# A fifth ranked job transposed, and four row blocks' gate logits from bfloat16 parts made by GpSimd

## The chip, the core and the metric

The kernel runs on one core of a Trainium2 chip. The metric is the device time of one execution in microseconds, the median of several runs. A core has TensorE (matmuls, with an instruction that loads weights beside them), VectorE, ScalarE and GpSimd, which work side by side on the on-chip memory SBUF and on the banks PSUM into which TensorE writes, and SyncE, which issues the direct loads. The tables call them PE, PEld, DVE, ACT, POOL and SP.

## What is computed

Chunked attention, then a layer of eight experts that takes the best two for each token, then a layer of eight experts that takes the best one, with a capacity:

```
x = attention(q, k, v, mem_k, mem_v)             # 1536 tokens x 512
logits = x @ w_gate + log1p(exp(x @ w_noise)) * noise
for e in 8 experts:                              # each token goes to its best two
    h = relu(x[mask] @ w1[e])                    # 512 -> 1024
    out[mask] += weight * (h @ w2[e])            # 1024 -> 512
logits = out @ w_gate2                           # second layer: the best one only
expert = argmax(logits); weight = softmax(logits)[expert]
out2[i] = weight * (relu(out[i] @ v1[expert]) @ v2[expert])   # first 384 tokens of an expert
```

The second gate picks by a maximum, so its logits have to be as exact as float32 makes them. A row of `out` is the sum of two experts' rows, and so are its logits.

## The kernel before

**Jobs.** After the attention stage the kernel runs jobs one after the other. A job is one expert's rows with its two layers. `V0` is a small block of the first rows in plain float32, and `V8` is an expert whose rows are known early (312 rows). `S0` to `S6` are the other seven experts of the first layer, sorted by their load while the kernel runs, with room for 432, 412, 404, 396, 384, 384 and 384 rows. `U0`, `UL` and `R0` to `R6` are the jobs of the second layer. `run_jobs` goes through them; `units()` of the class `Job` lists a job's units of work, and TensorE meets them in that order. Between units, `due` puts in the splits of weights that a plan gives for this unit, the blocks of the next job's input (`x_block`), and hooks such as the start of a gather.

**Three products for one.** A matmul of a job is made of three: weights and rows are each split into a high and a low part (`whi` and `wlo`, `xh` and `xl`, `hh` and `hl`), and `mm3` (L850 to L861) adds high by high, high by low and low by high. `split` (L785 to L798) makes the weights' parts: ScalarE copies a quarter of a block of 512 columns to the high part (L795), and VectorE subtracts it for the low part (L796); for the pieces named in `job.pool` GpSimd subtracts in its place. For V8 this is piece 3 of each weight block. The first layer's result gets its high part from ScalarE (`hh`, L872) and its low part from VectorE (`hl`, L873). The weights themselves come by SyncE's queue in halves (`half`, L764 to L776).

**Two kinds of job.** Kind "W" keeps the result transposed: layer 2 has eight units, one for each 128 of the 512 columns and half of the layer, its result is copied to `yh` (ScalarE, L888) and `yl` (VectorE, L889), and later `y_block` (L1055 to L1074) takes each block of 128 rows through eight matmuls of 144 columns, 128 of which turn it back into rows and 16 of which are the gate's logits. These blocks come in the next job's first layer, one behind a unit. Kind "M" makes rows directly: `rows2` for each block of 128 rows in two halves, then `weighted` (L1012) multiplies each row by its weight, `row_columns` (L1022) transposes the block by four matmuls (L1027) and ScalarE copies it to `yt` (L1028), `row_logits` (L1030) takes four float32 products for the logits (L1034), VectorE copies them beside the row (L1035), and `scatter` (L1037) lets GpSimd start the indirect transfer that adds the block to the table of rows (L1041). `Job.rows` (L1138) puts the two steps `row_columns` and `put` on a list, `todo`, from which `run_jobs` takes one after each unit.

**Which job is what.** A ranked job is "W" where its room is over 384, so S0 to S3 are; S4, S5 and S6 are "M". V0 is "T", a third kind of one block in float32.

**What stands around S4.** At its end `job.late` runs `overflow_done`: the queue of routing steps is emptied, and all engines read a counter and branch (L1278 to L1281) over a loop, `rest1`, for rows that did not find room. The loop is not run with these inputs. It uses the buffers `st["y"]` (`yh`, `yl`) and the PSUM bank A. A hook at S5's unit 3 starts `choose`, whose loads tell which experts the second layer has.

## Time and profile before

| | us |
|---|---|
| median of three runs | 598.04 |
| lowest and highest of these | 596.28 and 598.69 |
| the profiled execution | 597.38 |
| its span, first to last instruction | 595.5 |
| TensorE busy, matmuls | 582.8 (98%) |
| TensorE busy, weight loads | 519.4 (87%) |
| VectorE busy | 369.9 (62%) |
| ScalarE busy | 303.6 (51%) |
| GpSimd busy | 171.9 (29%) |

The profile is one execution on the chip. An engine is busy while it runs an instruction that computes; branches, semaphores and the issue of DMAs are not counted. The shares are averages over the whole span, over stages with different limits. TensorE's granted clock was 0.999 of its full 2.4 GHz over the span. A float32 matmul is recorded as two instructions, so the four float32 products of a block's logits are eight records.

In the rows below, a line of the trace names the line of the kernel, the engine's operation, the result and the operands (`wlo<-raww,whi`), and the shape as partitions by elements. L796 is the line 796 that the listing above shows. Where a row says what ended a wait, the operation behind the arrow is the one that was waited for.

### The profile page before, as it was taken

Reading aid. Unit: us, or ns where it says so; the run is one execution under the profiler, and the core shown is the slowest. Engines: PE = TensorE matmul, PEld = TensorE weight load, DVE = VectorE, ACT = ScalarE, POOL = GpSimd, SP = SyncE. Lnnn points to the kernel's source line nnn. Section 1 sums busy time; section 2 is a strip of 40 time slices with the busy share of each in tenths; the row PEclk is TensorE's granted clock in tenths of the full one; section 3 lists DMA queues with packets and bytes.
Section 4 is the critical chain, followed back from the end, with each engine's and each line's share of the span. In section 5 each row is a group of like instructions: output and inputs, shape, how many; then the busy total and the mean of one; then the engine's idle time right before and its main releaser. Section 6 shows DMA issues by size and latency. Waiting matters only on the chain. (4 is left out here: it accounts for less than half of the span.)

```text
span 595.5 us, 12285 instructions
## 1 busy us (share of the span) xinstructions
PE 582.8 (98%) x4547; PEld 519.4 (87%) x4547; DVE 369.9 (62%) x977; ACT 303.6 (51%) x638; POOL 171.9 (29%) x248
## 2 busy tenths in 40 slices
PE   8999999999999999999999999999999999999996
PEld 5798766899999999999998898988979978879984
DVE  7788757966466555555555257373668648457662
ACT  5764534355455445445355345344327657467562
POOL 8896104245114114213030311203341111220110
PEclk9999999999999999999999999999999999999999
DMA  9995747365767648556455563544376576975750
GB/s 263 281 203 157 250 138 245 113 214 168 228 202 184 199 155 213 165 140 165 143 122 162 134 166 138 110 143 125 40 249 221 193 263 227 390 265 175 249 175 25
DMA packets 75293, 110.13 MB, mean 185 GB/s; under 512 B 28083, under 2 KB 28083, under 8 KB 75226
## 3 DMA queue, kind: packets, MB, share of 16 engines
q1 hardware_dynamic: 65866, 84.72, 44.9%
q0 software_dynamic: 9360, 24.54, 17.6%
q8 instruction: 38, 0.62, 0.5%
q14 instruction: 29, 0.24, 0.1%
HBM read 88.63 MB, written 20.48 MB: 183 GB/s over the span
## 5 line engine op out<-in xcount | busy, mean ns | idle before, releaser
L796 DVE TENSOR_TENSOR wlo<-raww,whi 128x512 fp32r<-128x512 f32 x223 | 149.5, 693 | 39.2 <-ACT whi L795 37.6
L795 ACT ACTIVATE whi<-raww 128x512 fp32r<-128x512 f32 x228 | 135.6, 623 | 3.3 <-SPq L1372 1.4
L873 DVE SCALAR_TENSOR_TENSOR hl<-psA,hh 128x256 fp32r<-128x256 f32 (+7 forms) x104 | 53.4, 514 | 77.1 <-ACT hh L872 76.8
L872 ACT ACTIVATE hh<-psA 128x256 fp32r<-128x256 f32 (+7 forms) x104 | 47.4, 455 | 102.3 <-PE psA L861 102.0
L861 PE MATMUL psA<-xh,wlo 128*128 128x256 f32 (+7 forms) x416 | 84.8, 325 | 2.0 <-DVE hl L873 1.0
L861 PE MATMUL psA<-xl,whi 128*128 128x256 f32 (+7 forms) x416 | 82.2, 319 | 0.0
L861 PE MATMUL psA<-xh,whi 128*128 128x256 f32 (+7 forms) x416 | 82.2, 319 | 0.0
L1041 POOL DMA_INDIRECT x_rows<-yr,ids x25 | 39.3, 1571 | 123.6 <-ACT whi L795 86.2
L861 PEld LDWEIGHTS psA<-xh,wlo 128*128 128x128 f32 x416 | 66.5, 188 | 4.2 <-DVE hl L873 2.2
L861 PEld LDWEIGHTS psA<-xl,whi 128*128 128x128 f32 x416 | 68.1, 188 | 0.5 <-DVE xl L813 0.2
L861 PEld LDWEIGHTS psA<-xh,whi 128*128 128x128 f32 x416 | 68.2, 188 | 0.3
L801 POOL DMA_INDIRECT xg<-x_rows,ids x37 | 37.2, 1005 | 95.4 <-DVE gs L1081 39.8
L861 PE MATMUL psC<-wlo,hh 128*128 128x512 f32 (+1 forms) x184 | 52.7, 406 | 0.0
L861 PE MATMUL psC<-whi,hh 128*128 128x512 f32 (+1 forms) x184 | 51.3, 396 | 0.0
L861 PE MATMUL psC<-whi,hl 128*128 128x512 f32 (+1 forms) x184 | 50.1, 394 | 0.0
L813 DVE TENSOR_TENSOR xl<-psB,xh 128x512 fp32r<-128x512 f32 (+4 forms) x32 | 20.4, 638 | 35.8 <-ACT xh L812 35.7
L861 PEld LDWEIGHTS psC<-whi,hl 128*128 128x128 f32 (+1 forms) x184 | 34.1, 186 | 8.1
L861 PEld LDWEIGHTS psC<-whi,hh 128*128 128x128 f32 (+1 forms) x184 | 33.8, 186 | 8.1
L861 PE MATMUL psA<-hh,wlo 128*128 128x312 f32 (+4 forms) x160 | 37.0, 352 | 0.1
L1048 POOL DMA_INDIRECT out_dram<-yr,oids x12 | 11.9, 994 | 87.1 <-ACT yr L1017 53.6
L861 PEld LDWEIGHTS psC<-wlo,hh 128*128 128x128 f32 (+1 forms) x184 | 32.1, 186 | 5.6
L812 ACT ACTIVATE xh<-psB 128x512 fp32r<-128x512 f32 (+4 forms) x32 | 17.8, 555 | 37.6 <-PE psB L809 35.4
(371 smaller groups left out, 935.2 us busy)
## 6 DMA issues: line engine op xcount, KB each, us to landing
raww<-in_moe_w_dram SPq DMA_DIRECT2D x114, 512.0 KB
raw<-in_k_dram SPq DMA_DIRECT2D x6, 512.0 KB
raw<-in_q_dram SPq DMA_DIRECT2D x6, 512.0 KB
x_rows<-xs SPq DMA_DIRECT2D x12, 256.0 KB
out_dram<-zero SPq DMA_DIRECT2D x3, 1024.0 KB
...
```

What stands on the lines that cost most here:

```text
L795: nc.scalar.activation(hi[:, c], raw, AF.Copy)
L796: (eng or nc.vector).tensor_tensor(lo[:, c], raw, hi[:, c], op=OP.subtract)
L801: return nc.gpsimd.indirect_dma_start(out=xg, out_offset=None, in_=src, in_offset=bass.IndirectOffsetOnAxis(ap=ids_ap, axis=0))
L812: nc.scalar.activation(xh[:, :, o], pv[:, :, 0:n], AF.Copy)
L813: low = lambda: nc.vector.tensor_tensor(xl[:, :, o], pv[:, :, 0:n], xh[:, :, o], op=OP.subtract)
L861: nc.tensor.matmul(ps, w[a], x[b], start=first and i == 0, stop=last and i == n - 1)
L872: nc.scalar.activation(hh[:, f, 0:C], ps[:, 0:C], AF.Relu)
L873: nc.vector.scalar_tensor_tensor(hl[:, f, 0:C], ps[:, 0:C], 0.0, hh[:, f, 0:C], op0=OP.max, op1=OP.subtract)
L1041: wr = nc.gpsimd.indirect_dma_start(out=x2_d, out_offset=off, in_=yr[:n], in_offset=None, compute_op=OP.add)
L1048: wr = nc.gpsimd.indirect_dma_start(out=out, out_offset=off, in_=yr[:n, 0:DM], in_offset=None, bounds_check=N - 1, oob_is_err=False)
```

## The change

It has three parts.

1. **S4 becomes transposed.** The first five ranked jobs are "W", whatever their room. S4's row blocks then go through `y_block` in S5's first layer, behind the branch. As `yh` and `yl` hold S4's result across the branch, `rest1` gets two buffers of its own and the PSUM bank C. The hook that starts `choose` moves from S5's unit 3 to its unit 5.
2. **Four blocks' logits from three bfloat16 parts.** For V0's block, for two blocks of S5 and for the first of S6 (`job.parts`), the transposed rows in `yt` are split by `three` into three bfloat16 parts: a cast, a subtraction to a remainder, a cast of that, and a second subtraction, each on 128x512, all on GpSimd. The gate's weights get the same three parts once, in `wg3`, side by side in 24 columns. Twelve matmuls (three parts by four pieces of 128) with 24 columns take the place of the four float32 products, and one reduction by VectorE of the three sums in place of its copy. The parts lie where `hr` was, the remainder in `h0`, which hold a part of V0 and are free behind it. For such a block `put` moves: it is kept until just before the next block's transposes, or, for the last of them, two empty entries stand between the transposes and `put`.
3. **V8's weights.** `V8.pool` goes from `(3,)` to `(1, 3)`: GpSimd subtracts two of the four pieces of each of V8's weight blocks.

```diff
--- before.py
+++ after.py
@@ -197,6 +197,8 @@
     noi = axp.tile([128, NT, V], F32, name="noi")
     wg1 = consts.tile([128, KD, 2 * V], F32, name="wg1")
     wg2 = consts.tile([128, KD, E], F32, name="wg2")
+    wg3 = consts.tile([128, KD, 3 * E], BF, name="wg3")
+    wgr = consts.tile([128, KD, E], F32, name="wgr")
 
     def xs(t):
         if t not in xb:
@@ -401,6 +403,14 @@
             nc.vector.tensor_copy(yid[:, :, i, 128:136], wg2)
         nc.vector.tensor_tensor(yid[:, :, 0, 136:144], wg2, yid[:, :, 0, 128:136], op=OP.subtract)
         nc.vector.tensor_copy(yid[:, :, 1, 136:144], zero[:, 0:32].rearrange("p (k e) -> p k e", k=KD))
+        three([wg3[:, :, E * i:E * i + E] for i in range(3)], wg2, wgr)
+
+    def three(b, x, r):
+
+        nc.gpsimd.tensor_copy(b[0], x)
+        nc.gpsimd.tensor_tensor(r, x, b[0], op=OP.subtract)
+        nc.gpsimd.tensor_copy(b[1], r)
+        nc.gpsimd.tensor_tensor(b[2], r, b[1], op=OP.subtract)
 
     def all_of(gen):
 
@@ -1019,17 +1029,27 @@
             nc.vector.tensor_scalar(yr[:n, m:DM], ps[:n, m:DM], g[:n], None, op0=OP.mult)
         return yr
 
-    def row_columns(yr, n):
+    def row_columns(yr, n, parts=False):
 
         p = bank("B")
         pv = p.rearrange("p (k n) -> p k n", k=KD)
         for k in range(KD):
             nc.tensor.transpose(pv[:, k, 0:n], yr[:n, 128 * k:128 * k + 128], ident[:n, :n])
         nc.scalar.activation(st["yt"][:, :, 0:n], pv[:, :, 0:n], AF.Copy)
-
-    def row_logits(yr, n):
+        if parts:
+            three(st["y3"], st["yt"], st["h0"][0])
+
+    def row_logits(yr, n, parts=False):
 
         p = bank("D")
+        if parts:
+            for k in range(KD):
+                for i in range(3):
+                    nc.tensor.matmul(p[:n, 0:3 * E], st["y3"][i][:, k, 0:n], wg3[:, k],
+                                     start=k + i == 0, stop=k == KD - 1 and i == 2)
+            nc.vector.tensor_reduce(yr[:n, DM:W2], p[:n, 0:3 * E].rearrange("p (s e) -> p e s", s=3),
+                                    axis=AX.X, op=OP.add)
+            return
         for k in range(KD):
             nc.tensor.matmul(p[:n, 0:E], st["yt"][:, k, 0:n], wg2[:, k], start=k == 0, stop=k == KD - 1)
         nc.vector.tensor_copy(yr[:n, DM:W2], p[:n, 0:E])
@@ -1107,6 +1127,8 @@
             self.pool = ()
             self.weigh = 1 if kind == "T" else 5
             self.prev = []
+            self.parts = 0
+            self.put = None
             self.g = []
 
         def fetch(self):
@@ -1148,10 +1170,21 @@
             n = min(128, self.C - 128 * blk)
             yr = weighted(st["l2"], self.g[blk], n, self is R[-1])
             if self.first:
+                parts = blk < self.parts
+
                 def put():
-                    row_logits(yr, n)
+                    row_logits(yr, n, parts)
                     scatter(yr, n, self.ids[blk], True, self.prev)
-                self.todo += [lambda: row_columns(yr, n), put]
+                before, self.put = self.put, put
+
+                def columns():
+                    if before is not None:
+                        before()
+                    row_columns(yr, n, parts)
+                self.todo.append(columns)
+                if blk == self.nb - 1 or not parts:
+                    self.todo += [lambda: None] * (2 if parts else 0) + [put]
+                    self.put = None
                 return
             f = lambda: scatter(yr, n, (self.oids or self.ids)[blk], False, self.prev)
             if self.oids is None:
@@ -1272,7 +1305,7 @@
             nc.vector.tensor_reduce(ei, er, axis=AX.X, op=OP.add)
         return nc.sync.value_load(ei[0:1, 0:1], min_val=0, max_val=E - 1)
 
-    def rest1(wa, wb, ov, en, nb, after):
+    def rest1(wa, wb, ov, en, nb, hi, lo, after):
 
         fl, idf, nvi = ov
         n = nc.values_load(nvi[0:1, 0:1], min_val=0, max_val=V * nb)
@@ -1286,20 +1319,19 @@
                 x_block(xg, 0, 128)
                 g = wp["A"].tile([128, 1], F32, name="gs", bufs=10)
                 gate1(xg, se, g)
-                hi, lo = st["y"]
 
                 def part(src):
 
                     raw = b_.tile([128, 4, 256], F32, name="oraw", bufs=1)
                     nc.sync.dma_start(raw, src)
-                    nc.scalar.activation(hi[:, :, 0:256], raw, AF.Copy)
-                    nc.vector.tensor_tensor(lo[:, :, 0:256], raw, hi[:, :, 0:256], op=OP.subtract)
-                    return [(hi[:, k, 0:256], lo[:, k, 0:256]) for k in range(4)]
+                    nc.scalar.activation(hi, raw, AF.Copy)
+                    nc.vector.tensor_tensor(lo, raw, hi, op=OP.subtract)
+                    return [(hi[:, k], lo[:, k]) for k in range(4)]
 
                 xh, xl = st["x"]
                 for f in range(4):
                     ws = part(wa[ds(r, 1)].rearrange("e (k p) f -> p (e k) f", p=128)[:, :, 256 * f:256 * f + 256])
-                    ps = bank("A")
+                    ps = bank("C")
                     mm3(ps[:, 0:256], [((xh[:, k, 0:128], xl[:, k, 0:128]), ws[k]) for k in range(KD)])
                     nc.scalar.activation(st["hr"][:, 256 * f:256 * f + 256], ps[:, 0:256], AF.Relu)
                 for c in range(2):
@@ -1535,6 +1567,7 @@
     wp["B"] = pool("wpB")
     st["h"] = (wp["B"].tile([128, FB, CM], F32R, name="hh"), wp["B"].tile([128, FB, CM], F32R, name="hl"))
     st["hr"] = wp["B"].tile([128, FF], F32, name="hr")
+    st["y3"] = [st["hr"].bitcast(BF)[:, 512 * i:512 * i + 512].rearrange("p (k n) -> p k n", k=KD) for i in range(3)]
     st["yt"] = wp["B"].tile([128, KD, 128], F32, name="yt")
     st["hf"] = st["yt"].rearrange("p k (j n) -> p (k j) n", n=64)
     st["h0"] = wp["B"].tile([128, 4, 128], F32, name="h0"), st["yt"]
@@ -1542,8 +1575,7 @@
 
     whole3()
     n2 = 4 * E
-    kind1 = lambda c: "W" if c > 384 else "M"
-    S = [Job(kind1(caps1[1 + s]), 4 + 4 * s, caps1[1 + s], True) for s in range(E - 1)]
+    S = [Job("W" if s < E - 3 else "M", 4 + 4 * s, caps1[1 + s], True) for s in range(E - 1)]
     kind2 = lambda c: "T" if c <= 128 else "M"
     U0 = Job("M", n2, caps2[0], False, gate=lambda xg, g: gate2(xg, None, g))
     UL = Job("T", n2, caps2[E], False, gate=U0.gate)
@@ -1806,7 +1838,10 @@
 
         drain()
 
-        rest1(w1a, w2a, ov[1], en1, NB1, lambda: x_block(S[5].xg[0], 0, S[5].C))
+        op = pool("op", "right")
+        hi, lo = (op.tile([128, KD, 256], F32R, name="ow" + m) for m in "hl")
+        rest1(w1a, w2a, ov[1], en1, NB1, hi, lo, lambda: x_block(S[5].xg[0], 0, S[5].C))
+        pools["op"].close()
 
     hooks = {}
     bg["gen"], bg["next"] = chain(), bg["credit"]
@@ -1824,8 +1859,8 @@
         hook(S[j], 4, lambda j=j: blank_rows(*zeros2[j]))
     hook(V8, 10, lambda: run_until(lambda: S[0].xg))
     V8.turns = [11, 12, 13, 14]
-    V8.pool = (3,)
-    hook(S[-2], 3, behind(choose))
+    V8.pool = (1, 3)
+    hook(S[-2], 5, behind(choose))
     hook(S[-1], 3, behind(early))
     hook(S[-1], 12, lambda: run_until(lambda: U0.xg))
     hook(U0, 3, behind(chain2))
@@ -1846,11 +1881,13 @@
 
     hook(V0, 1.5, meanwhile)
     hook(V0, 3, weights8)
-    assert S[4].kind == "M" and S[5].kind == "M"
+    assert S[5].kind == "M"
     S[4].late = overflow_done
     U0.late = drain
     U0.weigh = UWE
     U0.pool = (1, 3)
+    for job, m in ((V0, 1), (S[5], 2), (S[6], 1)):
+        job.parts = m
     S[0].quiet = S[-1].quiet = U0.quiet = 0
     U0.turns = [2 * U0.nb + 6.5]
     S[-1].turns = [12, 12.5]
```

The first place is GpSimd between V0's end and V8's first units. `raww` is a half of raw weights (the memset orders its load), `wlo` and `whi` are low and high weights, `xg` gathered rows; the row from L1041 is V0's scatter. Before:

```order
L774 MEMSET raww 1x1 x2
L1039 MEMSET spacer 1x1
L1041 DMA x_rows<-yr,ids_e 1664x520
L796 TENSOR_TENSOR wlo<-whi 128x512
L796 TENSOR_TENSOR wlo<-raww,whi 128x512
L801 DMA xg<-x_rows,ids_2172 128x521 x4
L796 TENSOR_TENSOR wlo<-raww,whi 128x512 x2
L1039 MEMSET spacer 1x1
```

After; L410 to L413 are `three`, `hr` holds the parts and `h_1699` (that is `h0`) the remainder:

```order
L784 MEMSET raww 1x1 x2
L410 CAST hr<-yt 128x512
L411 TENSOR_TENSOR h_1699<-yt,hr 128x512
L412 CAST hr<-h_1699 128x512
L413 TENSOR_TENSOR hr<-h_1699,hr 128x512
L806 TENSOR_TENSOR wlo<-whi 128x512 x2
L1059 MEMSET spacer 1x1
L1061 DMA x_rows<-yr,ids_e 1664x520
L806 TENSOR_TENSOR wlo<-raww,whi 128x512 x2
L811 DMA xg<-x_rows,ids_2190 128x521 x4
L806 TENSOR_TENSOR wlo<-raww,whi 128x512 x4
```

V0's four operations stand in front of all subtractions of V8, and V0's scatter, which was ahead of the first subtraction, stands behind two. The gathers of S0 (`xg`) are behind four subtractions where they were behind two.

The second place is TensorE from the branch at S4's end into S5. `xh`, `xl`, `whi`, `wlo` make the first layer; three such rows are a unit of twelve matmuls. Before:

```order
L1280 UNCONDITIONAL_BRANCH x2
L861 MATMUL psA<-xh,wlo 128x384 x4
L861 MATMUL psA<-xl,whi 128x384 x4
L861 MATMUL psA<-xh,whi 128x384 x4
L861 MATMUL psA<-xh,wlo 128x384 x4
L861 MATMUL psA<-xl,whi 128x384 x4
L861 MATMUL psA<-xh,whi 128x384 x4
L1027 MATMUL psB<-ident,yr 128x128 x4
L861 MATMUL psA<-xh,wlo 128x384 x4
L861 MATMUL psA<-xl,whi 128x384 x4
L861 MATMUL psA<-xh,whi 128x384 x4
L1034 MATMUL psD<-wg_120,yt 128x8 x4
```

After; the matmuls of 144 columns are S4's `y_block`, with `yid` the identity and the gate's weights beside it:

```order
L1313 UNCONDITIONAL_BRANCH x2
L871 MATMUL psA<-xh,wlo 128x384 x4
L871 MATMUL psA<-xl,whi 128x384 x4
L871 MATMUL psA<-xh,whi 128x384 x4
L871 MATMUL psA<-xh,wlo 128x384 x4
L871 MATMUL psA<-xl,whi 128x384 x4
L871 MATMUL psA<-xh,whi 128x384 x4
L1086 MATMUL psC<-yid,yh 128x144
L1087 MATMUL psC<-yid,yl 128x144
L1086 MATMUL psC<-yid,yh 128x144
L1087 MATMUL psC<-yid,yl 128x144
```

Before, the transposes and float32 logits of S4's last block lie between S5's units; after, the first of S4's row blocks comes behind the second unit, and no transposes are left there.

The third place is TensorE in S5, from a block's transposes to its logits. `psB<-ident,yr` are the block's transposes, `psB<-ident,xg` those of the next job's input, `psC` is layer 2. Before:

```order
L1027 MATMUL psB<-ident,yr 128x128 x4
L809 MATMUL psB<-ident,xg 128x128 x4
L861 MATMUL psC<-wlo,hh 128x512 x4
L861 MATMUL psC<-whi,hh 128x512 x4
L861 MATMUL psC<-whi,hl 128x512 x4
L1034 MATMUL psD<-wg_120,yt 128x8 x4
L861 MATMUL psC<-wlo,hh 128x512 x4
L861 MATMUL psC<-whi,hh 128x512 x4
L861 MATMUL psC<-whi,hl 128x512 x4
L1027 MATMUL psB<-ident,yr 128x128 x4
L861 MATMUL psC<-wlo,hh 128x512 x4
L861 MATMUL psC<-whi,hh 128x512 x4
```

After; `hr` holds the bfloat16 parts of the block, and `ums,ones` is a matmul of the routing that happens to lie there:

```order
L1037 MATMUL psB<-ident,yr 128x128 x4
L819 MATMUL psB<-ident,xg 128x128 x4
L871 MATMUL psC<-wlo,hh 128x512 x4
L871 MATMUL psC<-whi,hh 128x512 x4
L871 MATMUL psC<-whi,hl 128x512 x4
L1702 LDWEIGHTS ones
L1702 MATMUL psD<-ums,ones 128x8
L871 MATMUL psC<-wlo,hh 128x512 x4
L871 MATMUL psC<-whi,hh 128x512 x4
L871 MATMUL psC<-whi,hl 128x512 x4
L1048 LDWEIGHTS hr
L1048 MATMUL psD<-wg_121,hr 128x24
```

One unit (12 matmuls of layer 2) lay between the transposes and the logits of a block; now two do, and the logits are twelve pairs of a weight load and a matmul of 24 columns, of which the first stands last in the fence.

## Rows read from the trace of the kernel before

**Rows 1.** TensorE's waits over the whole span: us in total, times, longest

```profile
PE psA L861 <- DVE hl L873: 1.0, 2, 0.5
...
PE psA L861 <- ACTq L1280: 0.3, 1, 0.3
```

**Rows 2.** busy us and instructions of each engine in V8's first half, clock, DMA

```profile
105.10:117.50 12.40, 11.18 (x82) 9.97 (x82) 12.21 (x27) 5.37 (x11) 3.00 (x2) 1.00 0.39 104
```

**Rows 3.** TensorE in order of time, V8: start, us, instruction, what ended its wait

```profile
102.31 0.60 PE L1027 MATMUL psB<-ident,yr 128*128 128x128 f32 x4
...
111.99 0.84 PE L861 MATMUL psA<-xh,wlo 128*128 128x312 f32 x4 [0.51 <-DVE hl L873]
...
116.59 0.69 PE L861 MATMUL psA<-hh,wlo 128*128 128x312 f32 x3
```

**Rows 4.** VectorE in order of time, V8's first half

```profile
109.36 2.18 DVE L474 TENSOR_TENSOR oh_L<-iot,oh_lo 128x1024 f16<-128x1024 f16 x1
111.46 0.47 DVE L873 SCALAR_TENSOR_TENSOR hl<-psA,hh 128x312 fp32r<-128x312 f32 x1
...
114.92 1.22 DVE L474 TENSOR_TENSOR oh_L<-iot,oh_lo 128x1024 f16<-128x1024 f16 x1
116.06 0.48 DVE L873 SCALAR_TENSOR_TENSOR hl<-psA,hh 128x312 fp32r<-128x312 f32 x1
```

**Rows 5.** GpSimd in order of time, V8, S5 and S6

```profile
108.77 1.68 POOL L796 TENSOR_TENSOR wlo<-whi 128x512 fp32r<-128x512 f32 x1
...
376.83 1.57 POOL L1041 DMA_INDIRECT x_rows<-yr,ids  x1 [5.20 <-DVE yr L1035]
...
404.40 0.98 POOL L801 DMA_INDIRECT xg<-x_rows,ids_u  x1 [0.30 <-issue]
```

**Rows 6.** all subtractions of line 796: ns min/median/max, first and last start

```profile
L796 DVE TENSOR_TENSOR wlo<-raww,whi x223: 672/691/1721, 111.9 to 582.2; 128x512 fp32r<-128x512 f32 x112
...
L796 POOL TENSOR_TENSOR wlo<-raww,whi x5: 1282/1286/1624, 117.5 to 424.3; 128x512 fp32r<-128x512 f32 x5
```

**Rows 7.** GpSimd's copies of line 140, the same columns

```profile
L140 POOL COPY v<-v x46: 606/614/829, 14.8 to 53.7; 32x520 f32<-32x520 f32 x46
```

**Rows 8.** TensorE in order of time, S3's row blocks and S4's first layer

```profile
305.85 0.23 PE L1066 MATMUL psC<-yid,yh 128*128 128x144 f32 x1
...
306.69 0.90 PE L861 MATMUL psA<-xh,wlo 128*128 128x384 f32 x4
...
311.55 0.86 PE L861 MATMUL psA<-xh,wlo 128*128 128x384 f32 x4
...
313.64 0.86 PE L861 MATMUL psA<-xh,wlo 128*128 128x384 f32 x4
```

**Rows 9.** TensorE in order of time, the end of S5, and S6

```profile
371.73 0.60 PE L1027 MATMUL psB<-ident,yr 128*128 128x128 f32 x4
372.08 1.17 PE L861 MATMUL psC<-wlo,hh 128*128 128x512 f32 x4
...
374.93 0.95 PE L1034 MATMUL psD<-wg,yt 128*128 128x8 f32 x8
375.74 0.95 PE L861 MATMUL psA<-xh,wlo 128*128 128x384 f32 x4
...
400.48 0.46 PE L529 MATMUL psD<-ol_R3l,ol_Ll 128*128 128x3 f16 x12
400.80 0.71 PE L861 MATMUL psC<-wlo,hh 128*128 128x512 f32 x2
...
406.43 0.95 PE L1034 MATMUL psD<-wg,yt 128*128 128x8 f32 x8
```

**Rows 10.** groups by line and shape: busy us, mean ns; idle before, releaser

```profile
L889 DVE TENSOR_TENSOR yl<-psA,yh 128x396 fp32r<-128x396 f32 x4 | 2.3, 571 | 4.0 <-ACT yh L888 4.0
...
L888 ACT ACTIVATE yh<-psA 128x396 fp32r<-128x396 f32 x4 | 2.0, 502 | 5.9 <-PE psA L861 5.9
```

**Rows 11.** ScalarE's copies of line 1028: ns min/median/max

```profile
L1028 ACT ACTIVATE yt<-psB x10: 597/598/602, 103.0 to 415.9; 128x512 f32<-128x512 f32 x10
```

## The prediction

> **What bounds the kernel now.** I read the waits of TensorE first, then TensorE's own order of time in the three stages that the change touches, then VectorE and GpSimd in the same stages. The waits [rows 1] are few and short: the two longest that concern the changed stages are 1.0 us for VectorE's `hl` (twice 0.5) and 0.3 us at the branch in front of S5. So nearly everywhere TensorE goes from one group of matmuls to the next, and a microsecond taken from its stream is a microsecond of the kernel; a wait put into its stream likewise. There is one exception, the first half of V8, from 105.1 to 117.5 us [rows 2]: VectorE is busy 12.21 of 12.40 us there and TensorE 11.18, and TensorE's units start right when a VectorE operation ends. `hl` ends at 111.46 + 0.47 = 111.93 and the unit starts at 111.99; `hl` ends at 116.06 + 0.48 = 116.54 and the unit starts at 116.59 [rows 3, 4]. In this stretch VectorE sets the pace, in all others TensorE.
>
> **The fifth ranked job, S4, transposed.** As rows, each of its three blocks costs TensorE four transposes and four float32 products. The transposes take 372.08 - 371.73 = 0.35 us, the products 375.74 - 374.93 = 0.81 us [rows 9]: 1.16 us a block. Transposed, a block costs the eight 144-column matmuls, 306.69 - 305.85 = 0.84 us [rows 8]. That is 3 x (1.16 - 0.84) = 1.0 us less. The layer itself has the same number of columns: 12 matmuls of 384 take 313.64 - 311.55 = 2.09 us [rows 8], eight such units 16.7; 12 of 512 take 374.93 - 372.08 = 2.85 [rows 9], six such units 17.1, but this 2.85 stands behind transposes, so I count only 0.1 of the difference. TensorE saves 1.1 us.
>
> The branch takes it back. What is late there now is short, 0.3 us [rows 1]: behind the last block's matmuls TensorE still had float32 products to do while ScalarE weighted the rows. As a transposed job, S4 ends with its last matmul, and behind it, before the other engines reach the branch, come ScalarE's copy `yh` (0.50) and VectorE's `yl` (0.57) [rows 10], and behind those the weight piece of unit 15, whose subtraction is 0.69 [rows 6]. S5's first matmuls wait for ScalarE to have passed the branch and the second group for VectorE. Copy, subtraction, subtraction and the 0.3 of the branch make 2.1 us from TensorE's last matmul; the first group of S5, a third of a 2.09 unit, may run in the last part of it. So 2.1 - 0.7 = 1.4 us idle where 0.3 was, a loss of 1.1. Queued behind the waiting matmul is all of S5. Bounds: 0.5 if the weight piece is out of the way early, 1.7 if nothing overlaps. **Sum for S4: 0.0 us** (-0.6 to +0.6). The scatters of S4 now stand behind S6's gathers on GpSimd, and the two loads of `choose` go out on SyncE's queue two units later, with the weight loads behind them; the first that needs their result is U0, more than a whole job on, so I give this nothing. S5's and S6's own units cover it; if they didn't, one load would show.
>
> **Four blocks from bfloat16 parts.** The float32 products (0.81) give way to twelve 16-bit matmuls. The nearest rows are twelve float16 matmuls with 128x128 weights and 3 columns: 400.80 - 400.48 = 0.32 us [rows 9]. Ours have 24 columns; I take 0.33, so 0.48 us less a block. S5's two blocks and S6's one save 1.45 us together. V0's block lies in the stretch that VectorE paces, so there its 0.48 is worth nothing.
>
> The price is GpSimd's four operations on 128x512 a block: two casts, two subtractions. A subtraction of this size is 1.28 [rows 6]. A cast is not in the trace; the nearest row is a copy of 520 float32 at 0.61 [rows 7], and I take 0.61 (from 0.3, half the bytes written, to 1.28, the subtraction). One block: 2 x 0.61 + 2 x 1.28 = 3.8 us (3.2 to 5.1). All four wait for each other. The logits come two TensorE units after the transposes, and the question is whether GpSimd is done by then.
>
> S5, block 0: from the transposes to the logits are 0.35, as much for an `xg` block, and two units of 2.85: 6.4 us. GpSimd starts after the transposes (0.60 [rows 9]) and ScalarE's `yt` (0.60 [rows 11]), and some 0.1 on: 1.3 + 3.8 = 5.1; with two or three VectorE subtractions in between (why they count comes below) 6.5 to 7.1. A wait of 0.3. S5, block 1: GpSimd must first scatter block 0. Scatter began 376.83 - 374.93 = 1.9 us after the float32 logits began [rows 5, 9], some 0.5 sooner with short ones, and is 1.57 long: it ends 3.0 after the logits, 2.6 after block 1's transposes; 3.8 more makes 6.4. TensorE wants the parts after 0.35 + 2.85 + 2.09 = 5.3. A wait of 1.1. S6, block 0: the two gathers of U0 stand ahead on GpSimd's queue, the second until 404.40 + 0.98 = 405.4 [rows 5]; 3.8 more and one or two VectorE subtractions make 409.9 to 410.6. The logits, at 406.43 before [rows 9], move one unit of 2.85 on to 409.3. A wait of 1.2 is more likely than none, 0.6 to 1.8. Together 2.6 us of waits against 1.45 saved: **+1.1 us** (-1.45 with no wait, +2.5 with slow casts).
>
> **V8, where VectorE paces.** Here the change takes two subtractions off VectorE (piece 1 of two weight blocks, 2 x 0.69 = 1.4 us) and puts on GpSimd those two (2 x 1.28) and V0's four operations (3.8): 6.4 us. What such company costs shows in the rows of before. GpSimd's subtraction at 108.77 is 1.68 long, to 110.45; VectorE's one-hot of 1024 starts at 109.36 beside it and takes 2.18, while the same operation at 114.92, with GpSimd idle, takes 1.22 [rows 4, 5]. So 0.96 us were lost out of 1.09 that the two lay side by side. The longest of VectorE's 223 subtractions is 1.72 against a median of 0.69, and GpSimd's own reach 1.62 to 1.68 against 1.28 [rows 6]. The `hl` at 111.46 and its like, which read PSUM, keep their 0.47.
>
> The Trainium skill, page "SBUF — State Buffer", section "Who interferes with whom", says that a VectorE instruction with two SBUF inputs and a GpSimd instruction that reads SBUF exclude each other for a whole instruction, and that the later one waits in full. The trace agrees (0.96 of 1.09). If the two only shared the port, half of the loss would be right, and the sum below would be about 1.4 us smaller.
>
> By the rows, then, I lay the operations end to end. V0's parts begin at 102.31 + 0.60 + 0.60 + 0.1 = 103.6 [rows 3, 11]; the first cast and subtraction (1.9) are through by 105.5, before VectorE's dense stretch. Left in the stretch are 6.4 - 1.9 = 4.5 us of GpSimd operations that exclude most of VectorE's, less the 1.4 taken off: 3.1. Some of it hides behind the `hl`, pieces of 0.47 [rows 4], of which one or two lie where GpSimd has work waiting: 0.3 to 0.9. Against this, ScalarE's next weight copy waits for GpSimd's last subtraction of the block before, and `hh` stands behind it. I take **+2.8 us**. Bounds: -1.4, if GpSimd's work costs VectorE nothing and only the relief is left; +4.5, if nothing hides and the relieved places stay empty because VectorE waits for ScalarE there.
>
> The parts of the gate weights (four operations on 128x32, once, while GpSimd has finished its copies), the one reduction in place of a copy of each block's logits and the two other subtractions that move to GpSimd, in V8's second half where TensorE paces, I put at 0: work of TensorE covers them; were it gone, four operations would be under 1 us.
>
> **The sum.** The profiled execution took 597.38 us (span 595.5 and 1.9 around it). 597.4 + 0.0 + 1.1 + 2.8 = 601.3. The median of the three runs is 0.7 above that execution; I forecast 601.5, between the two levels.
>
> **The rivals.** *Rival A, the covers hold.* VectorE's operations slip in between GpSimd's, the casts are short (0.3), and only a small part of the V8 price is paid, +0.7; the three waits shrink to 0.9 in all, so -0.5 there: 597.6 us. For it: six `hl` and the PSUM copies are free of conflict, and VectorE has idle time in S5 and S6. Against it: VectorE's 2.18 us at 109.36 [rows 4]. *Rival B, faster: VectorE's relief decides.* The place is V8's units u5 to u8, which wait for `hl`. If GpSimd's four operations for V0 are done before VectorE starts its long multiply and one-hot at about 108, the relief of 1.4 us counts in full; in S5 and S6 the parts are then in time too (-1.45), and S4 gains 0.6: 594.0 us. It decides from GpSimd needing under about 3 us a block. Against it: 2 x 1.28 alone is 2.6. *Rival C, the worst order.* Casts as slow as subtractions, 5.1 us a block: V8 +4.5, S5 and S6 +2.5: 604.4 us.
>
> **How the numbers follow.** Forecast 0.50, rival A 0.27, rival B 0.13, rival C 0.10. The range reaches from between A and B to C: 596.5 to 604.5. About 0.5% (3 us) is what a measurement of this kernel can tell from no change. The forecast lies 3.5 us above the median; some two tenths of the 0.50 (0.10) fall short of 3 us. Faster 0.13; same 0.27 + 0.10 = 0.37; slower 0.50. The likeliest case's own range is 600 to 603.
>
> **What would show it.** In V8: VectorE's one-hots and multiplies far above their lengths alone (1.22 for the one-hot) beside GpSimd's casts, and u8 starting about 3 us later. At S5's start: TensorE idle 1.2 to 1.6 us behind the branch. In S5 and S6: TensorE waiting for GpSimd in front of the 24-column matmuls, least at the first, some 1 us at the second and third. I am wrong if a GpSimd block is done in 3 us, if VectorE's operations keep their lengths beside it, or if TensorE's idle time at the branch stays at 0.3.

## The result: 603.74 us, 1.06% slower, within the range and 2.2 us above the forecast

The changed kernel takes 603.74 us (median of six runs, 602.86 to 605.30); the kernel before, on the same chips, 597.14 us. The ratio is 1.0106, with a 95% interval from 1.0091 to 1.0121. Against the kernel before, the forecast was +3.5 us and the measured change is +6.6. The profiled execution took 603.12 us, with a span of 601.3 and a mean granted clock of 0.991.

Where the time went is read best stage by stage. A stage is measured here from the start of TensorE's first matmul of a job to the first one of the next job, read from TensorE's rows in order of time. The start of V8 itself differs between executions by up to 2.8 us for reasons that lie in the attention stage, where the change adds only the four operations that make `wg3` (at 54.2 us, 0.2 us each on GpSimd); so the lengths of the stages say more than single totals.

| stage, us | before | changed | difference |
|---|---|---|---|
| V8 | 34.27 | 36.78 | +2.5 |
| S0 to S3 | 162.60 | 162.50 | -0.1 |
| S4 | 41.13 | 39.57 | -1.6 |
| S5 (with S4's row blocks) | 38.97 | 43.60 | +4.6 |
| S6 | 39.81 | 41.18 | +1.4 |
| U0 to the last matmul | 174.09 | 174.03 | -0.1 |

TensorE's waits in the changed kernel; the columns are those of [rows 1]. The two longest were not there before, and before there was one `hl` line with twice 0.5 us and 0.3 us at the branch:

```profile
PE psA L871 <- DVE hl L883: 3.6, 1, 3.6
PE psD L1702 <- DVE ums L1699: 2.5, 1, 2.5
PE psD L1048 <- POOL spacer L1059: 1.4, 2, 0.9
...
PE psA L871 <- DVE yl L899: 1.1, 1, 1.1
```

The first is V8's, the second S5's, the third is in front of the 24-column matmuls, the last is at the branch, where another 0.2 us follows. The view names `spacer` where the operation in front of it on GpSimd's queue, the last subtraction of the parts, is what was late. The third line's two places, TensorE in S6:

```profile
383.85 0.41 PE L1048 MATMUL psD<-wg,hr 128*128 128x24 bf16 x10 [0.93 <-POOL spacer L1059]
...
416.03 0.41 PE L1048 MATMUL psD<-wg,hr 128*128 128x24 bf16 x10 [0.49 <-POOL spacer L1059]
```

The first is S5's second block, whose logits now come in S6; the second is S6's first block.

**V8.** VectorE's rows of the changed kernel in order of time, chosen from V8's first half (start, us, engine, line, operation, shape, idle time before):

```profile
105.02 1.11 DVE L806 TENSOR_TENSOR wlo<-whi 128x512 fp32r<-128x512 f32 x1
...
106.24 2.26 DVE L455 TENSOR_TENSOR oh_pr<-oh,rk 128x72 f32<-128x72 f32 x2
...
108.88 0.79 DVE L465 TENSOR_SCALAR oh_hi<-oh_pi 128x16 int32<-128x16 int32 x1
...
111.27 0.48 DVE L883 SCALAR_TENSOR_TENSOR hl<-psA,hh 128x312 fp32r<-128x312 f32 x1
```

The same operations in the kernel before:

```profile
106.42 0.37 DVE L445 TENSOR_TENSOR oh_pr<-oh,rk 128x72 f32<-128x72 f32 x2
...
107.16 0.17 DVE L455 TENSOR_SCALAR oh_hi<-oh_pi 128x16 int32<-128x16 int32 x1
...
108.97 0.47 DVE L873 SCALAR_TENSOR_TENSOR hl<-psA,hh 128x312 fp32r<-128x312 f32 x1
```

GpSimd in the changed kernel, in order of time:

```profile
103.06 0.62 POOL L410 CAST hr<-yt 128x512 bf16<-128x512 f32 x1 [5.57 <-ACT yt L1038]
103.76 1.16 POOL L411 TENSOR_TENSOR h<-yt,hr 128x512 f32<-128x512 f32 x1
104.98 0.61 POOL L412 CAST hr<-h 128x512 bf16<-128x512 f32 x1
105.67 1.50 POOL L413 TENSOR_TENSOR hr<-h,hr 128x512 bf16<-128x512 f32 x1
107.14 2.50 POOL L806 TENSOR_TENSOR wlo<-whi 128x512 fp32r<-128x512 f32 x2
```

GpSimd works without a gap from 103.06 to 109.6. Beside it VectorE's two multiplies on 72 elements take 2.26 us, where the kernel before took 0.37 for the same two; `oh_hi`, on 16 elements, takes 0.79 instead of 0.17, and the subtraction at 105.02 1.11 instead of 0.69 [rows 6]. That is 1.89 + 0.62 + 0.42 = 2.9 us, and the `hl` for which TensorE stands still for 3.6 us ends at 111.75, 13.6 us behind V8's start; before it was 109.44, 10.7 behind it.

**S5.** TensorE, VectorE and GpSimd around the matmul of the choice, L1702, in order of time:

```profile
369.03 1.08 PE L871 MATMUL psC<-whi,hl 128*128 128x512 f32 x4
372.60 0.17 PE L1702 MATMUL psD<-ums,ones 128*128 128x8 bf16 x1 [2.48 <-DVE ums L1699]
372.62 2.05 PE L871 MATMUL psC<-wlo,hh 128*128 128x512 f32 x4
...
377.03 0.47 PE L1048 MATMUL psD<-wg,hr 128*128 128x24 bf16 x12
```

VectorE in the same stretch, in order of time:

```profile
366.65 0.24 DVE L1688 TENSOR_TENSOR gt<-gt,sel 128x84 f32<-128x84 f32 x1
...
367.86 0.55 DVE L440 TENSOR_TENSOR fm_e<-fm_e,rev 128x96 f32<-128x96 f32 x1
...
370.69 1.21 DVE L446 TENSOR_TENSOR uoh<-fm_e,fm_k 128x96 f32<-128x96 f32 x1
...
372.22 0.32 DVE L1699 TENSOR_REDUCE ums<-uoh 128x8 bf16<-128x96 f32 x1
```

GpSimd in the same stretch, in order of time:

```profile
367.60 0.69 POOL L410 CAST hr<-yt 128x512 bf16<-128x512 f32 x1 [15.29 <-ACT yt L1038]
...
370.30 1.48 POOL L413 TENSOR_TENSOR hr<-h,hr 128x512 bf16<-128x512 f32 x1
```

VectorE and TensorE in the kernel before, where the choice started at unit 3:

```profile
362.65 0.26 DVE L436 TENSOR_TENSOR uoh<-fm_e,fm_k 128x96 f32<-128x96 f32 x1
...
363.24 0.34 DVE L1667 TENSOR_REDUCE ums<-uoh 128x8 bf16<-128x96 f32 x1
...
364.00 0.18 PE L1670 MATMUL psD<-ums,ones 128*128 128x8 bf16 x1
```

TensorE has done all it could by about 370 and stands still until VectorE's `ums` is there at 372.54. L1702 adds up over the rows how many want each expert of the second layer, and the chain of small VectorE operations in front of it (from L1688 to L1699) lies on the same microseconds as GpSimd's four operations for S5's first block: `uoh` on 96 elements takes 1.21 us, where it took 0.26 before. The unit behind the wait then runs slowly; busy us, granted clock and DMA of both stretches:

```profile
107.70:111.80 4.10, 0.51 (x15) 0.38 (x13) 3.96 (x10) 1.06 (x2) 2.00 (x3) 1.00 0.00 0
111.80:116.87 5.07, 5.07 (x25) 5.07 (x25) 5.04 (x10) 0.95 (x2) 3.22 (x2) 0.66 0.18 18
370.10:372.60 2.50, 0.02 (x2) 0.00 (x1) 2.43 (x5) 1.72 (x3) 1.63 (x3) 0.99 0.02 6
372.60:377.03 4.43, 4.43 (x13) 3.35 (x13) 2.29 (x11) 0.00 (x0) 0.00 (x0) 0.62 0.19 69
```

The columns are length, busy time of TensorE, its weight loads, VectorE, ScalarE, GpSimd, then the clock. In the stretches where TensorE waits the granted clock is 0.99 or 1.00, and in those right behind them 0.66 and 0.62: for part of them TensorE had the lower of its two levels, 1.2 GHz. The unit that starts at 372.62 takes 4.4 us instead of 2.85 [rows 9]. The Trainium skill, page "TensorE: Matmul & The Clock Gate", section "HAM oscillation — how this bites in real kernels", describes a drop of this kind for a kernel whose TensorE waits for transfers: during the wait the clock is turned down, and the work behind it starts at the low level. These two rows agree in that; the experiments below show that the drop doesn't follow every wait of S5's length.

### The profile page after: what moved, and what is told of

It reads as the page before. It is cut to its first block, busy times and chain, and to the rows that moved or that the text cites. A ratio compares the mean times of both kernels' runs of the same rounds, so it can differ in the third digit from the quotient of the medians.

```text
span 601.3 us, 12381 instructions
## 1 busy us (share of the span) xinstructions
PE 580.6 (97%) x4575; PEld 520.5 (87%) x4575; DVE 378.8 (63%) x986; ACT 304.4 (51%) x642; POOL 193.8 (32%) x272
## 5 line engine op out<-in xcount | busy, mean ns | idle before, releaser
L871 PE MATMUL psC<-wlo,hh 128*128 128x512 f32 (+1 forms) x160 | 46.4, 410 | 0.0
L871 PE MATMUL psC<-whi,hh 128*128 128x512 f32 (+1 forms) x160 | 45.5, 401 | 0.0
L871 PE MATMUL psA<-hh,wlo 128*128 128x312 f32 (+5 forms) x192 | 44.0, 350 | 0.0
L871 PE MATMUL psC<-whi,hl 128*128 128x512 f32 (+1 forms) x160 | 43.5, 394 | 0.0
L871 PE MATMUL psA<-hl,whi 128*128 128x312 f32 (+5 forms) x192 | 41.9, 340 | 0.0
L871 PE MATMUL psA<-hh,whi 128*128 128x312 f32 (+5 forms) x192 | 41.9, 340 | 0.0
L871 PEld LDWEIGHTS psC<-whi,hh 128*128 128x128 f32 (+1 forms) x160 | 29.8, 189 | 7.1
```

The lines of the kernel that those rows point to most:

```text
L871: nc.tensor.matmul(ps, w[a], x[b], start=first and i == 0, stop=last and i == n - 1)
```

## The experiments

Each kernel is the changed one with the edit shown, unless it says otherwise. The lengths of the stages, in us, are of the profiled execution of each; the ratio is to the kernel before, with its interval, from executions of both on the same chip. S0 to S3 took 162.5 to 162.6 us in all of them.

| kernel | V8 | S4 | S5 | S6 | ratio |
|---|---|---|---|---|---|
| before | 34.27 | 41.13 | 38.97 | 39.81 | 1 |
| changed | 36.78 | 39.57 | 43.60 | 41.18 | 1.0106 (1.0091 to 1.0121) |
| 1 choice at unit 3 | 36.82 | 39.57 | 39.50 | 41.08 | 1.0058 (1.0040 to 1.0075) |
| 2 V8 and V0 as before | 34.08 | 39.57 | 41.76 | 41.20 | 1.0062 (1.0045 to 1.0079) |
| 3 no parts in S5, S6 | 37.87 | 39.57 | 40.66 | 39.71 | 1.0064 (1.0047 to 1.0081) |
| 4 S4 as rows | 36.79 | 41.05 | 41.97 | 41.36 | 1.0132 (1.0105 to 1.0159) |
| 5 V8's pieces alone | 34.93 | 39.57 | 42.03 | 41.15 | one execution |
| 6 V0's parts alone | 35.65 | 39.57 | 41.73 | 41.21 | one execution |
| 7 TensorE kept busy | 36.79 | 39.57 | 42.08 | 41.17 | one execution |
| 8 parts by other engines | 34.51 | 39.57 | 39.17 | 39.43 | 0.9985 (0.9971 to 1.0000) |
| 9 five blocks | 33.98 | 39.58 | 39.17 | 43.67 | 1.0045 (1.0027 to 1.0062) |
| 10 early piece | 34.80 | 39.50 | 39.01 | 43.35 | 1.0043 (1.0030 to 1.0055) |
| 11 five blocks, S4 as rows | 33.99 | 40.89 | 37.70 | 43.55 | 1.0043 (1.0029 to 1.0057) |
| 12 S4 as rows, four blocks | 33.99 | 40.70 | 37.57 | 39.54 | 0.9968 (0.9953 to 0.9982) |

### 1. The choice back at S5's unit 3

```diff
-    hook(S[-2], 5, behind(choose))
+    hook(S[-2], 3, behind(choose))
```

> The changed kernel, but with the hook that starts the choice of the second layer's experts back at S5's unit 3. Theory (the place of the choice): in the changed kernel TensorE waits 2.5 us in S5 for VectorE's `ums`, because its chain lies beside GpSimd's four operations for S5's first block, and TensorE's granted clock then drops for some 4.4 us, which costs another 1.6. Two units earlier the chain is done before GpSimd begins: the wait is under 0.5 us, no clock loss, S5 lasts 39.5 instead of 43.6 us, and the time is 603.7 - 4.1 = 599.6 us. Rival (late data): the choice waits for the loads behind S4's last scatter, which its place in the order does not move; then the wait stays at 2 us or more and the time at 603 us.

Measured: 600.56 us, S5 39.50 us, and no wait for `ums` at all. TensorE and VectorE of this kernel, in order of time:

```profile
367.43 0.18 PE L1702 MATMUL psD<-ums,ones 128*128 128x8 bf16 x1
...
374.24 0.46 PE L1048 MATMUL psD<-wg,hr 128*128 128x24 bf16 x12
```

VectorE in the same stretch, in order of time:

```profile
360.31 0.24 DVE L1688 TENSOR_TENSOR gt<-gt,sel 128x84 f32<-128x84 f32 x1
...
366.68 0.34 DVE L1699 TENSOR_REDUCE ums<-uoh 128x8 bf16<-128x96 f32 x1
...
372.26 0.96 DVE L1709 TENSOR_SCALAR sel_u<-ukey,umx 128x8 f32<-128x8 f32 x1
```

The chain is done at 367.0, before GpSimd's first cast (369.08), and its matmul slips into TensorE's stream. GpSimd's conflict is still there: it now hits `sel_u`, which takes 0.96 us (0.23 in the kernel before), but nobody waits for that. The rows of S4 were in time for the loads: the rival falls. In the profiles S5 is 4.1 us shorter. By the medians it is 3.2 us, and by the ratios (1.0106 to 1.0058) 2.9: part of the 4.1 is the clock's, which the profiled execution of the changed kernel paid; other kernels' executions with this wait did not all pay it (experiment 7), and how often the changed kernel does, one trace can't show.

### 2. V8 and V0 as before

```diff
-    V8.pool = (1, 3)
+    V8.pool = (3,)
-    for job, m in ((V0, 1), (S[5], 2), (S[6], 1)):
+    for job, m in ((S[5], 2), (S[6], 1)):
```

> The changed kernel, with V8 and V0 as before (GpSimd subtracts only piece 3 of V8's weights, V0's logits from float32 products); S4, S5, S6 as changed. Theory (GpSimd's work in VectorE's dense stretch costs V8 2.5 us): from V8's first matmul to S0's first 34.3 us as before, not 36.8, and 603.7 - 2.5 = 601.2 us. Rival (what V8 loses is made up elsewhere, since S0's inputs arrive when they arrive): 603 us or more, with S0 waiting for its gathers.

Measured: 599.72 us, V8 34.08 us. V8 gets back 2.7 us, and S0 does not give it away; by the ratios (1.0106 to 1.0062) it is 2.6. In this execution S5 was shorter too: its wait for `ums` is the same, the clock behind it is not (see 7).

### 3. No parts in S5 and S6

```diff
-    for job, m in ((V0, 1), (S[5], 2), (S[6], 1)):
+    for job, m in ((V0, 1),):
```

> The changed kernel, but without bfloat16 parts in S5 and S6 (float32 products and the copy there), V0 and V8 as changed, the choice still at S5's unit 5. Theory (GpSimd's conflict makes the chain of the choice late): three blocks cost 0.48 more each, +1.45, the two waits for GpSimd go, -1.4, and without GpSimd beside it the chain of the choice is 1.8 us shorter: TensorE's wait for `ums` falls from 2.5 to 0.7 us or less and the clock loss of 1.6 goes: 603.7 - 3.4 = 600.3 us. Rival (the place alone does it): the wait stays at 2 us or more and the clock drops, 603.7 us.

Measured: 600.20 us, no wait for `ums`. The choice is at unit 5 here, as in the changed kernel, and still its chain is in time: without GpSimd beside it, it takes from 368.09 to 372.14, 4.05 us, where the changed kernel takes 5.89 (366.65 to 372.54). The difference is the 1.8 expected. What helps too is that the float32 products of S5's first block stand in front of L1702 here and give VectorE 0.8 us more. VectorE in this kernel:

```profile
368.09 0.24 DVE L1688 TENSOR_TENSOR gt<-gt,sel 128x84 f32<-128x84 f32 x1
...
371.81 0.33 DVE L1699 TENSOR_REDUCE ums<-uoh 128x8 bf16<-128x96 f32 x1
```

So of the wait of 2.5 us at the later place, 1.8 are GpSimd's operations. The other 0.7, worked out from these rows, is the later place alone; it does not show here because the longer float32 products cover it. Experiment 1 ends the wait with GpSimd's operations still there. S5 and S6 together are 4.4 us shorter than in the changed kernel. V8 gives 1.1 back: it took 37.87 us here, since behind its wait of 3.6 us the clock was 0.58 over seven microseconds, against 0.76 in the other kernels with this V8.

### 4. S4 as rows

```diff
-    S = [Job("W" if s < E - 3 else "M", 4 + 4 * s, caps1[1 + s], True) for s in range(E - 1)]
+    S = [Job("W" if s < E - 4 else "M", 4 + 4 * s, caps1[1 + s], True) for s in range(E - 1)]
```

> The changed kernel with S4 as rows again (its hook for the choice still at S5's unit 5, parts and V8 as changed). Theory (transposing S4 saves TensorE some 1.1 us and gives 1.0 back at the branch): TensorE's wait at the branch is 0.3 us instead of 1.1 + 0.2, S4 and S5 together are 0.2 us longer, 603.9 us. Rival (the branch costs more than the transposition saves): 602.5 us. The wait for `ums` in S5 stays at 2 to 2.5 us with either.

Measured: 605.00 us; S4 and S5 together 83.02 us, against 83.17 with S4 transposed. The wait for `ums` stays at 2.5. The median and the ratio are above the changed kernel's (1.0132 to 1.0106, with intervals that overlap), but the stages don't show that: from V8's start to the last matmul this kernel's profiled execution takes 497.5 us and the changed one's 497.7; it only starts V8 1.9 us later, behind five microseconds of the attention stage (80 to 85) with the clock at 0.66. Transposing is worth nothing, within 0.2 us, as the theory had it; the 1.2 of the rival are not there. The wait at the branch is what gives the gain back; TensorE and VectorE of the changed kernel there:

```profile
337.00 0.97 PE L871 MATMUL psA<-xh,wlo 128*128 128x384 f32 x4 [1.14 <-DVE yl L899]
338.19 0.97 PE L871 MATMUL psA<-xl,whi 128*128 128x384 f32 x4 [0.23 <-DVEq L1313]
```

VectorE in the same stretch, in order of time:

```profile
336.42 0.56 DVE L899 TENSOR_TENSOR yl<-psA,yh 128x384 fp32r<-128x384 f32 x1 [2.38 <-ACT yh L898]
336.94 0.69 DVE L806 TENSOR_TENSOR wlo<-raww,whi 128x512 fp32r<-128x512 f32 x1
```

TensorE's first matmul of S5 starts as `yl` ends, 1.14 us idle, and the second group waits 0.23 more, until VectorE is through with the last weight piece and the branch.

### 5 and 6. V8's pieces alone, V0's parts alone

```diff
 5
-    for job, m in ((V0, 1), (S[5], 2), (S[6], 1)):
+    for job, m in ((S[5], 2), (S[6], 1)):
 6
-    V8.pool = (1, 3)
+    V8.pool = (3,)
```

> The changed kernel, with V0's logits from float32 products again; GpSimd still subtracts two pieces of each of V8's weight blocks. Read is V8, from its first matmul to S0's first: 34.27 us before, 36.78 changed, 34.08 with both undone. Theory (end to end: GpSimd's operations exclude VectorE's): the two subtractions move 1.4 us off VectorE and put 2.6 on GpSimd, V8 lasts 34.5 to 35.5 us, and without V0's four operations the long wait of 3.6 us for `hl` is gone. Rival (relief): VectorE has less to do and V8 is shorter than 34.0 us.

> The changed kernel, with GpSimd subtracting only piece 3 of V8's weight blocks as before; V0's logits from the bfloat16 parts. Read is V8's length. Theory (V0's four operations are the larger part of the loss): 35.5 to 36.5 us, with a wait for `hl` of 1.5 to 3 us around VectorE's operations on 72 elements, which GpSimd holds up. Rival (the moved subtractions are the larger part): under 35.2 us.

Measured: V8 takes 34.93 us with GpSimd's further subtractions alone, 35.65 with V0's parts alone, and 34.08 with neither. So the pieces cost 0.85, the parts 1.57, both 2.7. Each is one execution, and V8 as it was before took 33.98 to 34.80 us in experiments 2 and 8 to 12 (34.27 before): the 1.57 stands clear of that spread, the 0.85 hardly does. V0's parts are the larger share, though a part of theirs may be the clock: behind experiment 6's wait of 2.4 us it was 0.78 over seven microseconds, in experiment 5 1.00. Moving two pieces off VectorE brought no relief: in experiment 5 `oh_ev`, an operation of 0.22 us, takes 1.33 beside one of GpSimd's subtractions, more than the 0.69 that VectorE would have needed for the piece itself.

### 7. TensorE kept busy during the wait

```diff
         yield "pp"
+        warm(12)
         p = bank("D")
         nc.tensor.matmul(p[:, 0:E], ones, ms, start=True, stop=True)
```

> The changed kernel with twelve idle matmuls (128x512, bfloat16, of zeros) on TensorE ahead of the matmul that waits for `ums` in S5; they fill about the 2.5 us in which TensorE had nothing to do, and nothing else is changed. Theory (the clock falls because TensorE stood still): the next unit takes 2.85 us instead of 4.41, and S5 42.1 instead of 43.6 us. Rival (the clock falls for another reason, or the waiting is not what counts): S5 stays at 43.6 us, or is longer because the fillers come out behind `ums`.

Measured: S5 42.08 us, the unit behind the wait 2.9 instead of 4.4, with the clock at 1.00. That is the number of the theory. But the other kernels show that it proves less than it seems. The stretch of the wait and the unit behind it in experiment 2, which has the same wait and no fillers:

```profile
367.14:369.64 2.50, 0.03 (x1) 0.00 (x0) 2.43 (x5) 1.72 (x3) 1.64 (x3) 1.00 0.01 3
369.64:372.57 2.93, 2.93 (x13) 2.20 (x13) 2.30 (x11) 0.00 (x0) 0.00 (x0) 1.00 0.00 0
```

TensorE stood still for the same 2.5 us and the clock stayed at 1.00; likewise in experiments 5 and 6. In the changed kernel and in experiment 4 it fell to 0.62. So of five profiled executions with this wait two paid for it in clock, some 1.5 us, and three did not, nor did the one with the fillers. Behind V8's wait of 3.6 us, where nothing fills it, the clock fell in all five kernels that have it (changed, 1, 3, 4, 7). That standing still is the cause is in keeping with all of this; what decides at 2.5 us stays open.

### 8. The parts by ScalarE and VectorE

The choice at unit 3 and V8 and V0 as in experiments 1 and 2, and

```diff
-        nc.gpsimd.tensor_copy(b[0], x)
-        nc.gpsimd.tensor_tensor(r, x, b[0], op=OP.subtract)
-        nc.gpsimd.tensor_copy(b[1], r)
-        nc.gpsimd.tensor_tensor(b[2], r, b[1], op=OP.subtract)
+        nc.scalar.activation(b[0], x, AF.Copy)
+        nc.vector.tensor_tensor(r, x, b[0], op=OP.subtract)
+        nc.scalar.activation(b[1], r, AF.Copy)
+        nc.vector.tensor_tensor(b[2], r, b[1], op=OP.subtract)
```

> The changed kernel with three edits: the choice back at S5's unit 3, V8 and V0 as before, and the parts of S5's two blocks and S6's one made by ScalarE (two casts) and VectorE (two subtractions) instead of GpSimd. Theory (the parts pay where no operation of GpSimd's is on their way): no wait in front of the 24-column matmuls, S4 and S5 together 79.1 us (before 80.1), S6 39.6 (before 39.8, changed 41.2), V8 34.1: 1.4 us less than before, ratio 0.9977. Rival (the casts stand in ScalarE's queue in front of the copies of weights, and TensorE waits for weights or for the row weights): S5 and S6 together 2 us longer, ratio 1.002 to 1.003.

Measured: 596.02 us beside 597.16, ratio 0.9985, with the end of its interval at 1. S4 and S5 together take 78.74 us, S6 39.43. ScalarE, VectorE and TensorE for S5's first block:

```profile
365.53 0.63 ACT L410 ACTIVATE hr<-yt 128x512 bf16<-128x512 f32 x1
366.92 0.63 ACT L412 ACTIVATE hr<-h 128x512 bf16<-128x512 f32 x1 [0.76 <-DVE h L411]
```

VectorE in the same stretch, in order of time:

```profile
366.20 0.69 DVE L411 TENSOR_TENSOR h<-yt,hr 128x512 f32<-128x512 f32 x1 [0.54 <-ACT hr L410]
367.59 0.69 DVE L413 TENSOR_TENSOR hr<-h,hr 128x512 bf16<-128x512 f32 x1 [0.70 <-ACT hr L412]
```

TensorE in the same stretch, in order of time:

```profile
370.73 0.46 PE L1048 MATMUL psD<-wg,hr 128*128 128x24 bf16 x12
```

The parts are there 2.75 us after the start (365.53 to 368.28), and TensorE's twelve matmuls at 370.73 wait for nothing. On GpSimd the same block took 4.2 (367.60 to 371.78). The saving of 0.48 us a block is there once another engine makes the parts.

### 9 to 11. Five blocks, an early piece, and S4 as rows

From experiment 8: in 9 the parts also for S5's third block and S6's second one; in 10 besides that S4's last weight piece one unit earlier; in 11 instead of that S4 as rows.

```diff
 9
-    for job, m in ((S[5], 2), (S[6], 1)):
+    for job, m in ((S[5], 3), (S[6], 2)):
 10, besides
+        if job is S[4]:
+            us[15] = 14
 11, besides 9
-    S = [Job("W" if s < E - 3 else "M", 4 + 4 * s, caps1[1 + s], True) for s in range(E - 1)]
+    S = [Job("W" if s < E - 4 else "M", 4 + 4 * s, caps1[1 + s], True) for s in range(E - 1)]
```

> As the kernel with the parts made by ScalarE and VectorE (choice at S5's unit 3, V8 and V0 as before), but for all three blocks of S5 and two of S6. Theory (each block saves 0.48 us where its parts are in time): two more blocks, both with their logits in S6: S6 38.5 us against 39.4, S4 and S5 together 78.7 as there, and a ratio of 0.997 to the kernel before. Rival (S6's second block has only one unit between its transposes and its logits, and S5's third one stands among the first layer's `hh` on ScalarE): TensorE waits 0.5 to 1 us at either, and S6 stays at 39.4 us.

> The same kernel with five blocks, and the last piece of weights that is split in S4 moved from its unit 15 to its unit 14, so that ScalarE and VectorE have nothing left behind `yh` and `yl` when they reach the branch at S4's end. Theory (the branch waits for that piece): TensorE's second wait there, 0.2 us, goes and S4 and S5 together take 0.2 to 0.6 us less, 78.3 us. Rival (TensorE waits for `yl` alone): the 1.1 us stay and S4 and S5 together take 78.7 us.

> The kernel with five blocks, S4 as rows as in the kernel before. Theory (what transposing S4 saves the branch takes back): S4 and S5 together within 0.2 us of the 78.7 with S4 transposed, and the same ratio within 0.0015. Rival (transposing pays once nothing else disturbs S5): S4 and S5 together 79.5 us or more, as the four-block float32 products and transposes of rows cost 1.0.

Measured: 600.98, 600.47 and 600.99 us beside 597.89. S6 takes 43.4 to 43.7 us, 4 more than in experiment 8, and neither of the theories had that. VectorE, TensorE and SyncE's queue in experiment 9:

```profile
395.57 0.25 DVE L433 TENSOR_REDUCE fm_m<-lg 128x12 f32<-128x96 f32 x1 [3.49 <-DMA lg<-x_rows]
```

TensorE in the same stretch, in order of time:

```profile
397.96 0.18 PE L1733 MATMUL psD<-em,tri 128*128 128x12 bf16 x1 [2.51 <-DVE em L1729]
...
419.54 0.66 PE L1037 MATMUL psB<-ident,yr 128*128 128x128 f32 x4 [0.91 <-ACT yr L1027]
```

SyncE's queue in the same stretch, in order of time:

```profile
392.54 0.37 SPq L1678 DMA_DIRECT2D lg<-x_rows  x1
```

It is the mechanism of the choice once more. Early in S6 the kernel loads all logits (`lg`) and works out which rows come first in the second layer. The load has to wait for the scatter of S5's last block; its logits now come two units later, so the load goes out at 392.54, 16.3 us behind S6's start (12.0 in experiment 8), VectorE stands 3.5 us in front of `fm_m`, TensorE 2.5 us in front of L1733, and over the 6.5 us behind that the granted clock is 0.74. The rival had a part of it: the casts stand in front of `yr` on ScalarE, and S6's last transposes wait 0.9 us.

Experiment 10 puts the branch right by 0.24 us (78.51 against 78.75 for S4 and S5 together): TensorE's second wait is gone, and one of 1.07 stays. Experiment 11 repeats 4 without the disturbance: 78.59 us with S4 as rows, 78.75 transposed. It is 0.16 us, beside 0.15 in experiment 4.

### 12. What is left over: S4 as rows, four blocks by ScalarE and VectorE

From experiment 8:

```diff
-    S = [Job("W" if s < E - 3 else "M", 4 + 4 * s, caps1[1 + s], True) for s in range(E - 1)]
+    S = [Job("W" if s < E - 4 else "M", 4 + 4 * s, caps1[1 + s], True) for s in range(E - 1)]
-    for job, m in ((S[5], 2), (S[6], 1)):
+    for job, m in ((S[4], 1), (S[5], 2), (S[6], 1)):
```

> S4 as rows, the choice at S5's unit 3, V8 and V0 as before, and bfloat16 parts by ScalarE and VectorE for one block of S4, two of S5 and one of S6: none of them the last block of S5 or S6, on whose logits a load and a choice hang. Theory (0.48 us a block where parts are in time and nothing waits for the logits): S4 and S5 together 78.6 - 0.5 = 78.1 us (before 80.1), S6 39.4 (before 39.8), V8 34.1, ratio 0.996 to 0.998. Rival (the casts on ScalarE disturb S4's rows, or the logits' delay makes a choice late there too): a wait of over 0.5 us in S4 to S6, ratio 0.999 or more.

Measured: 595.73 us beside 597.33, ratio 0.9968 (0.9953 to 0.9982): faster than both kernels. S4 and S5 together take 78.27 us, S6 39.54. TensorE at S4's end:

```profile
331.14 0.46 PE L1048 MATMUL psD<-wg,hr 128*128 128x24 bf16 x12
...
336.14 0.97 PE L871 MATMUL psA<-xh,wlo 128*128 128x384 f32 x4 [0.48 <-ACTq L1313]
```

The 24-column matmuls of S4's block wait for nothing, and the branch costs 0.48 us of idle time instead of the 1.4 with S4 transposed.

## Why the prediction was right, and where it was not

**V8, right.** Forecast +2.8 us by laying GpSimd's and VectorE's operations end to end; measured +2.5 in the changed kernel, and 2.7 when both edits are undone in experiment 2 (2.0 to 2.8 by the six executions with V8 as before). The rows agree with the mechanism down to single operations, and the Trainium skill's rule (an operation of VectorE with two inputs in SBUF and one of GpSimd's that reads SBUF exclude each other, page "SBUF — State Buffer", section "Who interferes with whom") holds: two multiplies of 72 elements took 1.89 us longer beside GpSimd's 1.50 and 1.25. The price did not come where I looked for it, at the one-hots of 1024 elements (1.22 and 2.21 us, as before), but at the small operations ahead of them. What I had not thought of is the clock that falls behind the wait of 3.6 us. In the changed kernel VectorE was busy 5.04 of the 5.07 us behind it and set the pace anyhow, so the slow matmuls cost little; in experiment 3 they cost 1.1 us.

**S4, right.** Forecast 0.0 as 1.1 saved and 1.1 given back; measured +0.15 and +0.16 in two pairs. The idle time at the branch, forecast at 1.4 us, is 1.14 + 0.23. The step that named `yh`, `yl` and the last weight piece as the chain in front of it was right, and experiment 10 takes the piece's share away.

**The waits for the parts, mis-sized.** Forecast 0.3, 1.1 and 1.2 us; measured none that shows, 0.93 and 0.49 (none, 0.83 and about 0.5 in experiment 1, where nothing else disturbs S5). The term of S5 and S6 was to be +1.1 us net. In experiment 1, S4, S5 and S6 together take 120.15 us, 0.24 more than before, of which S4 is 0.15: the parts cost 0.1, not 1.1. What was too large is mainly S6's wait: GpSimd went straight from the second gather to the cast and needed 4.5 us, the low end of what I had worked out (3.8 and one subtraction of VectorE's). My own sum, 409.9 to 410.6 against 409.3, gives 0.6 to 1.3 there; I took 1.2, near its top.

**The step that failed: the choice.** I wrote of the loads of `choose` that the first to need their result is U0, more than a job on, and gave the move from unit 3 to unit 5 nothing. That followed the DMAs and the end of the chain, and skipped its middle. The first that needs the choice is TensorE itself, in S5, for the matmul L1702, and it stands in TensorE's order whether its data are there or not. It stood in the rows of the order that I showed, as a matmul of the routing between two units. Its cost was 2.5 us of waiting and, in the profiled execution, some 1.6 of low clock: 4.1 of the 6.8 us that the stages of the table lost (S5 43.60 against 39.50 in experiment 1). It is more than the whole distance to the forecast: the parts cost 1.0 less than I had said, the choice 3 to 4 more. I had the two facts that make it up in hand, the two units and the conflict with GpSimd, and used the second, for what VectorE loses by it, in V8 alone.

**What was luck.** The change cost 6.6 us and I had forecast 3.5, so the sum was too small by nearly half. That the time lies in the range, 0.8 us below its end, owes something to errors of opposite sign: the waits for the parts were put 1.0 us too high, and the kernel before ran at 597.14 us, 0.9 below the median that the forecast started from.

**The rivals.** The time lies between the forecast and rival C (604.4), but by none of C's reasons: GpSimd's cast is 0.61 us when it is alone, not 1.28, and V8 paid 2.5, not 4.5. C's +2.5 for S5 and S6 was itself too low: 1.3 us more a block on three waits would be 3.9 more. Rival B needs VectorE's relief, and experiment 5 shows none. Rival A was nearer than the forecast in S5 and S6 (-0.5 there, +0.1 measured), but its 0.7 for V8 is far off. None of the three signs that I named for being wrong came; I had named none for a wait of TensorE's at L1702.
